# Two constants of an issue order: gate rows made, stored and broadcast from a later point, and turned rows of the second batch counted as ready later

## The chip, the cores and the metric

The kernel runs on one core of a Trainium2 chip. A core has a matrix engine (PE, with its weight loads shown as PEld), a vector engine (DVE), a scalar engine (ACT), a GpSimd engine (POOL) and a sync engine (SP). Each engine works through its own instruction queue in order and waits on semaphores that others raise. Transfers are issued from the queues of POOL, SP and ACT and are carried by 16 DMA engines that all of them share. The metric is the device time of one execution, in microseconds (us).

## The reference

Attention with 4 sink keys and a window of 128 keys, over 4 batches, 8 heads, 768 positions and 64 channels; its output, as 3072 rows of 512 channels, goes through a mixture of 4 experts that are all computed for every row and added with weights (gates) that each row brings.

```python
scores = scale * np.matmul(q, k.transpose(0, 1, 3, 2))
keep = (pos[None, :] < n_sink) | ((rel >= 0) & (rel < window))
a = softmax(np.where(keep, scores, -1e9)); x = np.matmul(a, v)
p = domain_probs / (domain_probs.sum(-1, keepdims=True) + 1e-09)
for e in range(E):
    out += p[:, e:e + 1] * (np.maximum(x @ w1[e], 0.0) @ w2[e])
```

## The kernel before

**Tiling.** A batch is cut into 6 blocks of 128 rows, and two blocks make a group g of 256 rows, so there are 12 pairs (b, g). Attention of a pair takes, for each of 4 pairs of heads: scores (L684), exponentials on ACT (L709), masks on DVE (L703 or L718), the product with the values (L743 and L750), a division by the row sum (L777, then L780 on DVE in batch 0 or L789 on ACT), and a turn to channel-major (L808 with a copy at L270 in batch 0, a transposing DMA from SP later). The four sink keys have products of their own (`sinks`, L645), which need a group's q and k rows already turned. In batch 0, PE turns q and k; from batch 1 on a transposing DMA from SP does (`turn_nat`, L246).

**Experts.** A first product (weights w1) makes the hidden rows H, a second one (w2) the output. The first two pairs, (0,0) and (0,1), are "early": their first products are plain (L1058) or of the seven-product form (L1145), without gates, and their second products (L1397) multiply by the gate while they leave PSUM (L1407, L1409 on DVE). All other pairs multiply by the gate while H leaves PSUM (L1082 after plain products, L1178 after seven-product ones); their gates lie along the free axis and are the same on all partitions. Their second products are L1319. The seven-product forms need sums of weights, formed on DVE (L377 to L383 for w1, L341 to L347 for w2). A part of those for expert 2 lies in the same buffer as `scratch`, in which the gates are normalized.

**The gate rows.** `gates_by_row` does four DVE instructions on 24 partitions (a sum, an addition, a reciprocal, a product, L434 to L437) and two stores from SP into a buffer in DRAM (L441). `load_gates` then broadcasts one row of 256 gates to 128 partitions from there, for each pair and expert, with one DMA from SP (L457, 128 KB). It has 5 buffers: the first five broadcasts are issued at once, each later one when a pair and expert is finished. So the five rows of the first call are those of pair (0,2) with experts 0 to 3 and of pair (1,0) with expert 0.

**What sets the order.** The program writes out every engine's instructions once, in an order that a planner in the kernel chooses. It keeps a clock for each engine and queue in `t`, in ns by costs of its own, and in each turn of the main loop it emits for PE the piece of work that is ready first or has the best priority. Work of DVE and ACT is put into `pend` with a ready time and a deadline, and `flush` emits it up to PE's clock. Times of DMAs are estimated too: `lands` for loads from POOL, `sp` for DMAs from SP. The planner's clock decides the order alone; on the chip the waits are on semaphores.

Three places matter here. The main loop calls the gate rows once PE's clock has passed a constant:

```python
        if not rowed and now > ROWED:
            rowed = 1
            gates_by_row()
            load_gates()
```

`gates_by_row` books 2989 ns of DVE on the planner's clock by `dve(2800, 0.0)`, and `load_gate` books the SP queue, but the time at which a gate row lands is kept nowhere: the work at L1082 and L1178 counts as ready when its product is. The third place is the time at which a turned block of q and k rows counts as ready:

```python
        turned_at[b, tb] = sp(landed["qk", b, tb], scored_at.get(b - 1, 0.0),
                              issue=1330, takes=1400, turning=True) + LATE + ROWS1 * (b == 1)
```

`scores_ready`, `sinks_ready` and the step `keys` read it, so for batch 1 alone `ROWS1` says how much later these steps may be emitted. It also sets when the buffers of q and k rows count as free (`qkn_free`), and with that when loads of batch 2 are emitted and when three of the buffers are taken for expert 3's sums of w2 (`spare_rows`).

**Loads.** POOL issues all loads of q, k, v and weights in one order. Around the change they are: w1 of expert 1, w2 of expert 1, w1 of 2, w2 of 2, w1 of 3, then rows of batch 1, with w2 of 3 between them. Each weight load puts 1 MB into SBUF.

Of the kernel before, what the change touches and what calls it, by code (L numbers as in the profile page):

```python
# [16 lines left out]
def kernel(  # L17
# [63 lines left out]
    OPEN = 2.2  # L81
    SOON = 21000
    NEARLY = 2
    ROWED = 24000
    W2AT = 2
    ROWS1 = 1500
    ONACT = 1
    ONE = 2
    PAIR = 1
# [107 lines left out]
    def sp(*deps, issue=530, takes=600, turning=False):  # L197
        t["sp"] = max([t["sp"], *deps]) + issue
        at = max(t["hw"], t["sp"] + 800)
        row = next((x[3] for x in moved if x[1] <= at < x[2]), 0.0)  # L200
        if turning and row:
            t["hw"] = at + TURNED * (row + SHARE)
            t["sw"] += TURNED * SHARE
            for x in moved:
                if x[2] > at:
                    x[1] += TURNED * SHARE * (x[1] > at)
                    x[2] += TURNED * SHARE
                    landed[x[0]] = x[2] + 900
                    if x[0][0] == "w1" and ("w1", x[0][1]) in landed:
                        landed["w1", x[0][1]] = max(landed["w1", x[0][1]], x[2] + 900)  # L210
        else:
            t["hw"] = at + takes + max(0.0, min(takes, t["sw"] - at)) * (not turning)
        return t["hw"] + 900
# [28 lines left out]
    def turn_nat(b, tb):  # L242
# [6 lines left out]
        )  # L249
        turned_at[b, tb] = sp(landed["qk", b, tb], scored_at.get(b - 1, 0.0), issue=1330, takes=1400, turning=True) + LATE + ROWS1 * (b == 1)  # L250
        qkn_free.remove(1e12)
# [1203 lines left out]
    while mix.more() or att.more():  # L1455
        now = t["pe"]

        if not att.more() and ahead == B - 1 and not wide:
            wide = 1
            mix.widened()  # L1460
        if not rowed and now > ROWED:
            rowed = 1
# [107 lines left out]
```

## Time and profile before

| | |
|---|---|
| median of 3 runs | 361.21 us (360.98 to 362.25) |
| profiled execution, first to last instruction | 361.5 us |
| busy: PE, DVE, ACT, POOL | 351.5, 303.8, 162.4, 71.7 us |
| granted PE clock, mean | 0.999 |
| moved by DMA | 37.79 MB, mean 105 GB/s |
| the chain that ended last | PE 86%, DMA 11%, DVE 1% |

The profile is of one execution. "x8" counts instructions; a bracket behind an instruction says how long its engine stood idle before it and what released it. In the lists of waits, the numbers are the total in us, the times, and the longest. A DMA in the chain is counted from its issue to its landing. PE is busy nearly all the time, so a gap on PE, or work on PE that could be left out, is what the time can be read from.

### The profile page before, as it was taken

How to read it: one execution, taken by the hardware profiler on the slowest of the kernel's cores; microseconds unless marked ns; L12 is line 12 of the kernel's file. 1: busy time of each engine (PE TensorE's matmuls, PEld its weight loads, DVE VectorE, ACT ScalarE, POOL GpSimd, SP SyncE). 2: the span in 40 equal slices, each digit the busy share in tenths (PEclk: the TensorE clock that was granted, in tenths of full speed). 3: DMA queues.
4: the chain of work that ended last, by engine and by line, in shares of the span. 5: the costliest groups of instructions: out<-in, count | busy, mean ns of one | idle time of the engine just before them, and what ended most of it. 6: DMA issues, size and time to landing. Idle time of an engine off the chain costs nothing.

```text
span 361.5 us, 10704 instructions
## 1 busy us (share of the span) xinstructions
PE 351.5 (97%) x4476; PEld 302.4 (84%) x4484; DVE 303.8 (84%) x691; ACT 162.4 (45%) x414; POOL 71.7 (20%) x92
## 2 busy tenths in 40 slices
PE   8999989998999999999999999999999999999995
PEld 3575758766789898898899898899899999999984
DVE  6787969868799899699579999989879799899840
ACT  5854722447694373554544435345344432313110
POOL 8936012540356224001071000000000000000000
PEclk9999999999999999999999999999999999999999
DMA  9999999999999999217099712121310131110011
GB/s 165 171 180 194 232 210 180 156 146 169 176 133 173 162 157 135 61 47 86 19 158 173 126 65 55 31 75 16 60 62 28 31 76 60 31 58 4 3 60 59
DMA packets 117869, 37.79 MB, mean 105 GB/s; under 512 B 100676, under 2 KB 113316, under 8 KB 117820
## 3 DMA queue, kind: packets, MB, share of 16 engines
q0 software_dynamic: 77520, 17.31, 54.0%
q1 hardware_dynamic: 39244, 19.28, 27.8%
q8 instruction: 35, 0.57, 0.6%
q10 hardware_dynamic: 1056, 0.52, 0.5%
q14 instruction: 14, 0.11, 0.1%
HBM read 40.98 MB, written 6.34 MB: 131 GB/s over the span
## 4 chain that ended last, share of the span: by engine, by line
PE 86%; DMA 11%; DVE 1%; issue 1%; ACT 1%; POOL 0%; ACTq 0%; POOLq 0%; DVEq 0%
PE acc L1319 34%; PE cps L1145 32%; DMA w<-in_moe_w_dram 9%; PE hps L1058 7%; PE acc L1397 6%; PE sps L684 3%; PE od L750 2%; DMA kraw<-in_k_dram 2%; PE od L743 1%; PE sinks L645 0%; ACT aT L709 0%; POOL w L312 0%; DVE qkn L345 0%; DVE qkn L343 0%; ACT qkn L270 0%
## 5 line engine op out<-in xcount | busy, mean ns | idle before, releaser
L1145 PEld LDWEIGHTS <-w 128*128 128x128 bf16 x1184 | 72.5, 98 | 2.3 <-issue 0.9
L1319 PEld LDWEIGHTS <-H 128*128 128x128 bf16 x700 | 65.0, 98 | 8.0 <-issue 1.5
L1178 DVE SCALAR_TENSOR_TENSOR H<-cps,gates 128x512 bf16<-128x512 f32 x90 | 60.3, 679 | 0.1
L709 ACT ACTIVATE aT<-sps 128x512 bf16<-128x512 f32 (+1 forms) x96 | 46.9, 573 | 24.7 <-PE sps L684 24.6
L1319 PE MATMUL acc<-w,H 128*128 128x256 bf16 x420 | 55.4, 273 | 0.0
L1145 PEld LDWEIGHTS <-vf 128*128 128x128 bf16 x744 | 45.6, 98 | 1.2 <-issue 0.5
L1145 PE MATMUL cps<-T,w 128*128 128x128 bf16 x592 | 45.0, 219 | 0.0
L1058 PE MATMUL hps<-xT,w 128*128 128x256 bf16 x352 | 43.3, 273 | 0.9 <-DMA w<-in_moe_w_dram 0.9
L1145 PE MATMUL cps<-xT,w 128*128 128x128 bf16 x592 | 43.7, 219 | 0.0
L789 ACT ACTIVATE onat<-od,R 128x64 bf16<-128x64 f32 x144 | 33.2, 323 | 22.7 <-DVE R L777 22.6
L1191 ACT COPY cps<-cps 128x512 f32<-128x512 f32 x37 | 21.4, 578 | 42.1 <-PE cps L1145 27.5
L1058 PEld LDWEIGHTS <-w 128*128 128x128 bf16 x352 | 33.3, 98 | 6.6 <-DMA w<-in_moe_w_dram 1.2
L1369 ACT COPY osb<-acc 128x256 f32<-128x256 f32 x36 | 13.6, 377 | 50.7 <-PE acc L1319 50.7
L1145 PE MATMUL cps<-T,vf 128*128 128x128 bf16 x496 | 36.4, 219 | 0.0
L299 POOL DMA_DIRECT2D vx<-in_v_dram x24 | 21.6, 905 | 62.2 <-PE od L750 48.5
L1319 PEld LDWEIGHTS <-S 128*128 128x128 bf16 x320 | 30.4, 98 | 3.3 <-issue 0.2
L1397 PE MATMUL acc<-w,H 128*128 128x512 bf16 x120 | 29.3, 379 | 2.0 <-DMA w<-in_moe_w_dram 1.3
L1198 DVE TENSOR_TENSOR cps<-H,cps 128x512 f32<-128x512 f32 x32 | 22.1, 691 | 9.8 <-PE cps L1145 8.4
L1319 PE MATMUL acc<-wf,H 128*128 128x256 bf16 x208 | 29.3, 273 | 0.0
L703 DVE TENSOR_TENSOR aT<-aT,mask 128x1024 bf16<-128x1024 bf16 (+1 forms) x36 | 22.7, 640 | 4.3 <-ACT aT L709 4.0
L1213 DVE TENSOR_TENSOR H<-H,cps 128x512 f32<-128x512 f32 x32 | 21.8, 680 | 2.7 <-PE cps L1145 2.6
L1397 PEld LDWEIGHTS <-H 128*128 128x128 bf16 x128 | 12.1, 98 | 13.5 <-issue 1.7
(128 smaller groups left out, 546.2 us busy)
## 6 DMA issues: line engine op xcount, KB each, us to landing
w<-in_moe_w_dram POOLq DMA_DIRECT2D x7, 1024.0 KB, 18.3
out_dram<-osb SPq DMA_DIRECT2D x21, 256.0 KB
gates<-gate_rows SPq DMA_DIRECT2D x40, 128.0 KB
vx<-in_v_dram POOLq DMA_DIRECT2D x24, 128.0 KB, 7.0
qkn<-in_q_dram POOLq DMA_DIRECT2D x22, 128.0 KB, 8.8
qkn<-in_k_dram POOLq DMA_DIRECT2D x22, 128.0 KB, 9.8
w<-in_moe_w_dram POOLq DMA_DIRECT2D x2, 512.0 KB, 9.4
kraw<-in_k_dram ACTq DMA_DIRECT2D x2, 256.0 KB
```

The lines of the kernel that those rows point to most:

```text
L299: nc.gpsimd.dma_start(out=vx[tb][:, :, 0:D], in_=v[b, :, tb * P:(tb + 1) * P, :].rearrange("h p d -> p h d"),)
L703: nc.vector.tensor_mul(a, a, m[:, None, :].to_broadcast([P, 2, w]))
L709: nc.scalar.activation(out=a[:, ph], in_=sps[ph][:, 0:w], func=AF.Exp, scale=scale)
L789: nc.scalar.mul(o[:, qi, hp, ph * D:(ph + 1) * D], od[:, qi, ph, 0:D], R[:, qi, ph])
L1058: nc.tensor.matmul(h[:, i].rearrange("p (q n) -> p q n", q=2), lhsT=w1_sb[e][:, db, fb * P:(fb + 1) * P], rhs=xT[b, g][:, :, db], start=(i ...
L1145: nc.tensor.matmul(y[:, f], lhsT=A[:, d, f * P:(f + 1) * P], rhs=T[:, d], start=(m in ("P1", "P5") and f == 0 and d == 0), stop=(d == 1), ...
L1178: nc.vector.scalar_tensor_tensor(out=dst, in0=src, scalar=0.0, in1=gate, op0=ALU.max, op1=ALU.mult)
L1191: nc.scalar.copy(out=tiles["Y"], in_=y)
L1198: nc.vector.tensor_add(tiles["V"], c5, tiles["X"])
L1213: nc.vector.tensor_add(c5, c5, y)
L1319: nc.tensor.matmul(x, lhsT=self.operand(b, g, e, m)[:, f], rhs=forms[e][m][:, f], start=(k == 0 and f == 0 and m in (("P1", "P5", "P2") if ...
L1397: nc.tensor.matmul(op, lhsT=H[:, fb // QF, fb % QF, s], rhs=w2_sb[e][:, fb, :], start=(fb == 0), stop=(fb == NFB - 1),)
```

## The change

Two constants differ.

```diff
-    ROWED = 24000
+    ROWED = 38000
     W2AT = 2
-    ROWS1 = 1500
+    ROWS1 = 3500
```

With the first, the four DVE instructions, the two stores and the first five broadcasts of the gate rows are emitted when PE's planning clock has passed 38 us, not 24 us. With the second, the planner counts each of the six turned blocks of q and k of batch 1 as ready 2 us later than it did. No instruction is added or taken away by either; what else moves is what the planner orders differently because of them.

## The prediction

> **What bounds the kernel now.** I read the page first: PE is busy 351.5 of 361.5 us, so the time is PE's work plus PE's gaps. The list of PE's waits for named work has four gaps from 0.8 us up; one is at 1.4 us, before any of this, and the others are
>
> ```profile
> PE acc L1397 <- DMA w<-in_moe_w_dram: 1.3, 1, 1.3
> PE hps L1058 <- DMA w<-in_moe_w_dram: 0.9, 1, 0.9
> PE sinks L645 <- DVE qkn L345: 0.8, 1, 0.8
> ```
>
> The second is at 19.7 us, before either constant acts. Where the other two lie is seen in PE's timeline (start, duration, and in brackets the idle time):
>
> ```profile
> 43.86 1.04 PE L1058 MATMUL hps<-xT,w 128*128 128x256 bf16 x8
> 46.21 1.89 PE L1397 MATMUL acc<-w,H 128*128 128x512 bf16 x7 [1.32 <-DMA w<-in_moe_w_dram]
> ...
> 87.99 0.61 PE L1145 MATMUL cps<-xT,w 128*128 128x128 bf16 x8
> 89.45 0.29 PE L645 MATMUL sinks<-qkT,ksd 128*32 128x256 bf16 x4 [0.85 <-DVE qkn L345]
> ```
>
> Ends of matmuls are modelled, so I count by starts. Eight of 256 columns start 0.109 us apart, so the products at 43.86 free PE at 44.73: that gap is 1.48 us. The eight at 87.99 are through at about 88.4: 1.05 us. After 90 us I find no start on PE more than 0.25 us late against its columns. These two gaps, 2.5 us in all, are about what any reordering can win.
>
> The first gap's cause is in the chain, in order of time; expert 1's w2 lands at 46.17:
>
> ```profile
> 27.91 18.26 DMA w<-in_moe_w_dram
> 46.17 0.04 issue
> 46.21 0.38 PE acc L1397
> ```
>
> The weight landings of this queue are at 37.67, 46.17, 51.07, 56.15 and 61.16 us, so this 1 MB took 8.50 us and the next three 4.90 to 5.08. In between lie the gate rows (SP's timeline) and a DMA rate over its surroundings (windows: length, PE, PEld, DVE, ACT, POOL busy, clock, DMA share, GB/s):
>
> ```profile
> 27.96 1.72 SPq L441 DMA_DIRECT2D gate_rows<-scratch  x2
> 34.66 2.28 SPq L457 DMA_DIRECT2D gates<-gate_rows  x5
> ```
> ```profile
> 30.00:38.00 8.00, 7.84 (x70) 4.11 (x70) 6.39 (x13) 4.05 (x9) 3.98 (x6) 1.00 1.20 208
> 38.00:46.00 8.00, 6.82 (x93) 5.83 (x90) 7.72 (x24) 5.39 (x10) 0.83 (x1) 1.00 1.16 236
> 46.00:56.00 10.00, 9.68 (x64) 6.39 (x66) 6.25 (x11) 1.79 (x3) 1.75 (x2) 1.00 1.19 211
> 55.95:69.35 13.40, 13.35 (x181) 11.66 (x181) 13.26 (x22) 6.14 (x11) 7.22 (x8) 1.00 1.71 177
> ```
>
> The packets of the five broadcasts run from 38.0 to 46.1 us and put down 0.65 MB; meanwhile POOL's queue falls from 206 GB/s to between 135 and 177. The last window matters below: DVE is busy 13.26 of 13.40 us there.
>
> For the second gap the named releaser is chance: the weight load of L645 waits for the semaphores of two transposing DMAs, and the one issued at 79.51 (block 3 of batch 1) lands at 89.31.
>
> **The change, part 1: ROWED.** I take from the planner's clock only the order. It passes 38 us at 38.1, just ahead of the reciprocal that the trace has at 39.24. DVE's lines:
>
> ```profile
> 24.94 0.67 DVE L434 TENSOR_REDUCE scratch<-scratch 24x128 f32<-24x512 f32 x1
> ...
> 26.87 1.07 DVE L437 TENSOR_TENSOR scratch<-scratch 24x512 f32<-24x512 f32 x1
> ...
> 39.24 0.17 DVE L777 RECIPROCAL R<-od 128x4 f32<-128x4 f32 x1
> ...
> 53.36 0.69 DVE L1082 SCALAR_TENSOR_TENSOR H<-hps,gates 128x512 bf16<-128x512 f32 x1 [0.40 <-PE hps L1058]
> 53.97 0.68 DVE L377 TENSOR_TENSOR vf<-w 128x1024 bf16<-128x1024 bf16 x1
> 55.09 0.75 DVE L1409 SCALAR_TENSOR_TENSOR osb<-acc,scale_t,osb 128x512 f32<-128x512 f32 x1 [0.44 <-PE acc L1397]
> ```
>
> Removed at 24.94: 3.0 us of DVE (24.94 to 27.94). DVE idles 0.82 us right after, waiting for PE, so nothing is won. Two stores and five broadcasts leave the weight queue's way: w2 of expert 1 should take 5.0 us as its neighbours do and land at 37.67 + 5.0 = 42.7, before PE's 44.73. Gain 1.48 us.
>
> Added at 39.24: the same 3.0 us of DVE, to 42.2. Behind it queue masks, divisions and turns of batch 0. PE need not stand: the planner books the work, and has first products of (0,0) and (0,1) of expert 1 to put forward (w1 landed at 37.67). DVE's idle times up to 55.1 (1.32, 0.65, 0.78, 0.40, 0.44) are 3.59 us, 2.1 of them left if PE is 1.48 earlier; alone the block would leave DVE 0.9 us behind. If that cover were gone PE would lose the whole 3.0.
>
> SP's queue is empty from 8.4 to 60.5 us but for these transfers, and POOL's loads wait for none of them; both cost nothing.
>
> What the planner doesn't know is the landing of the rows. Before, DVE ended at 27.94 and row 0 landed at 40.07: 12.1 us, of which 6.7 for the stores (4.0 from issue to first packet) and 5.4 for the broadcast (3.3 to first packet). From 42.2 that gives 54.3; if the stores start as quickly as the broadcasts did, which met the same large weight packets, 53.6, which I take as the nearest row. Its first reader is the L1082 at 53.36, due 1.48 earlier, at 51.9. So DVE stands for 1.7 us, with evictions L1409 and weight sums queued behind. At 53.6 it is 0.24 behind its old times, regains the 0.44 of idle at 55.09, and from 55.96 to 69.35 has no idle to give: 0.20 ahead. PE leans on it there: the sum L1198 ends at 62.26 and the product that reads it starts near 62.6, a tolerance of 0.3. So PE keeps 0.5 of its 1.48: part 1 is **-0.5 us**. Ends: -1.48 if the rows are in time; +3.1 if row 0 takes the longest broadcast of the trace (issued 70.35, landed 78.61: 8.3 us), so 42.2 + 6.7 + 8.3 = 57.2 and 57.2 - 53.36 - 0.44 - 0.3.
>
> [...]
>
> **Part 2: ROWS1.** No instruction is added. Keys, scores and sinks of batch 1 come up to 2 us later in the order. `sinks` of group 1 is emitted as soon as block 3 counts as ready, so up to 2 us of other PE work (early products, second products) moves ahead of it. PE then reaches it at 88.4 - 0.5 + 2.0 = 89.9, after 89.31: **-1.05 us**. Ends: +0.0 if the piece put ahead must wait itself, -1.4 with the 0.32 us late start behind the scores at 89.85. The masks (L703) and expert 3's weight sums shift too; cover is DVE's idle time between 88.60 and 97.20, 8.60 less 5.63 busy, 3.0 us. If they land beyond it, where DVE is busy 10.00 of 10 us (100 to 110), up to 3.0 us can come back. I take 0 for this, since with the same booking rules no other order-made gap is in the trace after 90 us.
>
> **Sum.** -0.5 - 1.05 = -1.55 us. The profiled span, 361.5, is 0.3 over the median; I see nothing around it to count. 361.21 - 1.55 = 359.7 us. Faster or slower by 0.5% means under 359.4 or over 363.0.
>
> **The rivals.** *In time* (0.24): row 0 lands before about 52.5, DVE stays with PE and both gaps close: 361.21 - 1.48 - 1.05 = 358.7. For it: the broadcast issued at 143.32 landed at 146.41, 3.1 us; with that for both steps and 1.7 us to issue the stores row 0 lands at 42.2 + 1.7 + 3.1 + 3.1 = 50.1. Against: weight loads keep the DMA engines at 211 GB/s from 46 to 56, against 92 from 140 to 150.
>
> *Given back* (0.26): DVE work moved by the new order meets the full stretches 55.95 to 69.35 or 100 to 120, and PE waits there what it won: between 360.5 and, with the 3.0 us, 362.7; I put it at 361.3. It includes that ROWS1 only swaps one late transfer for another. For it: DVE at 84% of the span; against: PE has products to do whenever DVE is behind.
>
> *Rows late* (0.14), the slower side: PE's change from row 0's landing L is L - 54.1, with part 2 L - 55.15; over 1.8 us from L = 57.0 on. At 57.2 it is 361.21 + 2.05 = 363.3. For it: the 8.3 us row, and 5.6 for the row issued at 60.48; against: the 8.3 stood behind two transposes on SP's queue, and there are none before 60 us.
>
> **Numbers.** The forecast itself gets 0.36, with 359.0 to 360.5 as its own range, some 0.10 of it under 359.4. Faster 0.24 + 0.10 = 0.34. Slower: rows late and 0.06 of given back, 0.20. Same 0.46. Range 358.4 (in time, with the 0.32) to 363.1.
>
> **What would show it.** Landing of expert 1's w2 near 42.7 and no PE gap before L1397 there: else the broadcasts weren't what slowed it. First L1082 waiting for a gates DMA until 53 to 54.5: if it doesn't wait, "in time" holds; past 57, "rows late". PE less than 0.8 us ahead at 70 us. No gap before `sinks` near 90 us. PE without gaps over 0.5 us after 97. I'm wrong if the planner puts waits of other kinds into the first 100 us, above all for turned rows or weight sums.

## The result and the profile after

| | median, us | range | ratio to before, 95% interval |
|---|---|---|---|
| before, beside it | 361.63 | 360.93 to 362.69 | |
| changed | 364.01 | 363.83 to 364.73 | 1.0072 (1.0055 to 1.0090) |

The changed kernel is 0.7%, some 2.4 to 2.6 us, slower: outside the range, and on the other side. The profiled execution took 364.6 us, with a span of 362.9 us.

PE's waits for named work are the first view (total in us, times, longest). The waits for `w` before L1397 and before `sinks` that before had are gone, and a new one stands at the top:

```profile
PE cps L1145 <- DVE H L1082: 2.1, 1, 2.1
PE acc L557 <- DVE lent L468: 1.4, 1, 1.4
```

The chain shows where it comes from, in order of time (start, duration): DVE's gate instructions, the store, the broadcast of row 0, the first L1082, three more of them among other DVE work, and PE's product.

```profile
40.59 1.07 DVE scratch L437
...
42.65 5.18 DMA gate_rows<-scratch
47.82 0.02 SPq L457
...
47.87 7.02 DMA gates<-gate_rows
...
54.99 0.13 DVE H L1082
...
61.33 0.61 DVE H L1082
61.94 0.04 issue
61.98 0.27 PE cps L1145
```

From DVE's end at 41.66 to row 0's landing at 54.89 it is 13.2 us. DVE's timeline (start, duration; in brackets the idle time before, and its releaser) shows what that does:

```profile
50.58 0.69 DVE L383 TENSOR_TENSOR w<-w 128x1024 bf16<-128x1024 bf16 x1
54.99 0.69 DVE L1082 SCALAR_TENSOR_TENSOR H<-hps,gates 128x512 bf16<-128x512 f32 x1 [3.72 <-DMA gates<-gate_rows]
55.60 0.68 DVE L343 TENSOR_TENSOR wf<-wf,w 128x1024 bf16<-128x1024 bf16 x1
...
57.46 0.68 DVE L1082 SCALAR_TENSOR_TENSOR H<-hps,gates 128x512 bf16<-128x512 f32 x1
...
60.05 0.68 DVE L1082 SCALAR_TENSOR_TENSOR H<-hps,gates 128x512 bf16<-128x512 f32 x1
...
61.24 0.69 DVE L1082 SCALAR_TENSOR_TENSOR H<-hps,gates 128x512 bf16<-128x512 f32 x1
```

DVE has nothing it may do for 3.72 us, because the wait stands at the head of its queue; then it works without a gap until 65 us. Each of the four L1082 reads a PSUM tile that PE's next products need: six PSUM banks go round in this part of the kernel. PE's timeline shows the stop, until the last of the four has read its bank:

```profile
59.32 0.61 PE L1145 MATMUL cps<-xT,w 128*128 128x128 bf16 x8
61.98 1.86 PE L1145 MATMUL cps<-T,vf 128*128 128x128 bf16 x16 [2.05 <-DVE H L1082]
```

By starts PE is 2.22 us late there, and it was 0.50 us late before, at 58.87, where the profile names ACT's copy L1191, itself released by the second L1082. Two landmarks on PE give the balance, first in before, then in the changed kernel:

```profile
55.76 1.89 PE L1397 MATMUL acc<-w,H 128*128 128x512 bf16 x8
68.36 1.89 PE L1397 MATMUL acc<-w,H 128*128 128x512 bf16 x7
```
```profile
53.56 1.89 PE L1397 MATMUL acc<-w,H 128*128 128x512 bf16 x8
70.06 1.89 PE L1397 MATMUL acc<-w,H 128*128 128x512 bf16 x7
```

PE came 2.2 us ahead and left 1.7 us behind, so 3.9 us were lost in between. The two late starts are 2.7 us of it. Another 1.4 us are slower products: from 61.98 to 70.06 the changed kernel takes 8.08 us for what took before 6.68 us (61.68 to 68.36). A product of 0.2 us (L1153) that before has in this stretch is not in the changed profile. `sinks` is reached at 93.42 without a wait, and after 97 us no start of PE is more than 0.25 us late.

The slower products have their reason in the clock. In a table of windows (length; busy PE, PEld, DVE, ACT, POOL; granted clock, DMA share, GB/s) PE's clock falls to half during the stop, at 61.53, and stays there for 3.41 us:

```profile
60.00:61.00 1.00, 0.00 (x0) 0.00 (x0) 1.00 (x3) 0.16 (x1) 0.91 (x2) 1.00 2.43 155
61.00:62.00 1.00, 0.02 (x1) 0.02 (x1) 1.00 (x3) 0.41 (x1) 0.90 (x2) 0.77 2.39 158
62.00:63.00 1.00, 1.00 (x11) 1.00 (x10) 1.00 (x2) 0.00 (x0) 0.73 (x2) 0.50 1.82 184
63.00:64.00 1.00, 1.00 (x12) 1.00 (x11) 1.00 (x3) 0.58 (x1) 1.00 (x2) 0.50 1.29 210
```

By its mean clock the profiled execution is one of two among six that had this. The four others are slower than before as well, 363.83 to 364.07 us.

### The profile page after: what moved, and what is told of

It reads as the page before. It is cut to its first block, busy times and chain, and to the rows that moved or that the text cites. A ratio compares the mean times of both kernels' runs of the same rounds, so it can differ in the third digit from the quotient of the medians.

```text
span 362.9 us, 10709 instructions
## 1 busy us (share of the span) xinstructions
PE 353.8 (98%) x4475; PEld 304.3 (84%) x4483; DVE 302.2 (83%) x687; ACT 163.8 (45%) x418; POOL 71.9 (20%) x92
## 4 chain that ended last, share of the span: by engine, by line
PE 88%; DVE 4%; DMA 3%; ACT 2%; issue 1%; SPq 0%; DVEq 0%; ACTq 0%
PE acc L1319 34%; PE cps L1145 32%; PE hps L1058 8%; PE acc L1397 5%; PE sps L684 3%; PE od L750 3%; DMA gates<-gate_rows 2%; PE acc L557 2%; DMA gate_rows<-scratch 1%; ACT aT L709 1%; PE od L743 1%; DVE onat L780 1%; PE tr L578 1%; DVE H L1082 1%; DVE aT L718 1%
## 5 line engine op out<-in xcount | busy, mean ns | idle before, releaser
L1191 ACT COPY cps<-cps 128x512 f32<-128x512 f32 x37 | 21.6, 585 | 44.1 <-PE cps L1145 27.7
L1198 DVE TENSOR_TENSOR cps<-H,cps 128x512 f32<-128x512 f32 x32 | 22.2, 693 | 10.5 <-PE cps L1145 8.8
L1397 PE MATMUL acc<-w,H 128*128 128x512 bf16 x120 | 29.2, 379 | 0.5 <-issue 0.2
L1397 PEld LDWEIGHTS <-H 128*128 128x128 bf16 x128 | 12.2, 98 | 12.1 <-issue 0.2
```

Source lines behind the costliest of these rows:

```text
L1191: nc.scalar.copy(out=tiles["Y"], in_=y)
L1198: nc.vector.tensor_add(tiles["V"], c5, tiles["X"])
L1397: nc.tensor.matmul(op, lhsT=H[:, fb // QF, fb % QF, s], rhs=w2_sb[e][:, fb, :], start=(fb == 0), stop=(fb == NFB - 1),)
```

## The experiments

The theory was: DVE's wait for a late gate row costs the time, and nothing else in the change does. The rivals were the DVE block in its new place, the half clock, and ROWS1.

**The kernel before once more, and each constant alone.** The first has no edit; the others change one constant each:

```diff
-    ROWED = 24000
+    ROWED = 38000
```
```diff
-    ROWS1 = 1500
+    ROWS1 = 3500
```

> Nothing is changed. Theory: in the profiled execution of before, the loads of the first 25 us came late (expert 0's w2 landed at 27.63, and at 25.95 in the changed kernel's profile, where nothing before 24 us differs), so the 1.48 us gap before L1397 at 46.21 belongs to that execution. Then this profile shows expert 0's w2 landing near 26, a gap under 0.6 us there, a span near 360, and the gap before the sinks of batch 1 (1.05 us) still there. Rival: the gap is the kernel's own, from the broadcasts alone: expert 1's w2 8.5 us after w1, a gap of 1.3 to 1.5 us, whatever the start.

> The gate rows from 38 us, ROWS1 as before. Theory (row 0 lands near 55, DVE waits for it 3 to 4 us in order and PE loses it between 58 and 65): all of the loss is here, and ROWS1's gain of 1.0 is missing: 2.4 + 1.0 = 3.4 us over before. Rival (the loss comes from batch 1's later order): within 0.7 us of before.

> ROWS1 alone, the gate rows from 24 us. Theory: the gap before the sinks closes and nothing else opens: 1.0 us under before (0.7 to 1.3). Rival (the later order of batch 1 fills stretches in which DVE is full, and costs): 1 to 2.5 us over before.

| | median, us | ratio, 95% interval |
|---|---|---|
| before | 362.08 | |
| before again | 361.84 | 1.0003 (0.9988 to 1.0019) |
| ROWED alone | 364.51 | 1.0067 (1.0045 to 1.0088) |
| ROWS1 alone | 361.01 | 0.9978 (0.9962 to 0.9994) |

ROWED alone brings the loss, 0.67% (2.4 us), and its DVE timeline has the same wait:

```profile
51.08 0.69 DVE L383 TENSOR_TENSOR w<-w 128x1024 bf16<-128x1024 bf16 x1
55.62 0.69 DVE L1082 SCALAR_TENSOR_TENSOR H<-hps,gates 128x512 bf16<-128x512 f32 x1 [3.85 <-DMA gates<-gate_rows]
```

ROWS1 alone is 0.22% faster, 0.8 us by the ratio, and its profile has no gap before `sinks`. But the 3.4 us expected of ROWED alone did not come: the two constants together (1.0072) lose as much as ROWED alone (1.0067), so the gain of ROWS1 does not show beside a late row. In the profile of ROWED alone PE reaches `sinks` at 91.11 without a wait; it comes there so late that ROWS1 has no gap to close. The half clock is in this number too: five of the six executions of ROWED alone have it by their mean clock, with spans of 362.6 to 363.5 us, and the one without has 361.6 us. How much of the 2.4 us it is can't be told from one execution.

The new profile of before is the other finding. Its span is 359.5 us in an execution of 361.23 us, and PE's waits in it are:

```profile
PE acc L557 <- DVE lent L468: 1.4, 1, 1.4
PE sinks L645 <- DMA qkT<-qkn: 0.6, 1, 0.6
```

The second line names the transposing DMA as what `sinks` waits for, as the prediction had argued. The wait for w2 of expert 1, which the prediction meant to win back, is not there: w2 landed at 44.02, just ahead of PE. An execution takes its span and about 1.7 us (1.65 to 1.77 in 75 executions of before). The profiled execution of before, with 361.5 us of span, had therefore, worked out so, taken about 363.2 us, 1.6 to 2 us over the median. The gap comes and goes: four profiles have the gate rows from 24 us, and three of them have it (before, ROWS1 alone with 1.0 us in its list of waits, and the kernel below that does the DVE block twice, with 1.4 us). What repeats is the slow load behind it: in these four, w2 landed 7.2 to 8.5 us after w1. In the seven profiles with the rows from 31 us or later it landed 5.1 to 5.9 us after w1, and none has the gap.

**The rows in time.** The same edit, but at an earlier point, with ROWS1 at 3500:

```diff
-    ROWED = 38000
+    ROWED = 31000    # and 34500, and 36000
```

> The gate rows from 31 us, ROWS1 3500. Theory: DVE ends them near 35, row 0 lands 12 to 13 us later, near 48, before its first reader at 51 to 52: no wait of DVE for a gate row, the broadcasts mostly behind expert 1's w2. Time as ROWS1 alone or a little better, 1.0 to 1.7 us under before. Rival (it is the 3 us block on DVE amid batch 0's last masks, not the landing, that costs): 1 us or more over before.

> The gate rows from 34.5 us, ROWS1 3500. DVE ends them near 38, so row 0 lands near 51, about when its first reader comes (51.3). Theory (the cost begins where the landing passes the reader, and PE has some slack behind that): 0.5 to 1.2 us under before. Rival (the cost grows with every us of delay from 31 to 38): halfway, 0.7 us over before or more.

> ROWS1 at 3500, ROWED at 36000. On the queues this is the changed kernel with the DVE block about 1.7 us (one eviction, one reciprocal, one division, one mask) further ahead; the order behind it is nearly the same. The theory (PE pays for the time that DVE waits for row 0, and the row lands about 13.2 us after the block's end) expects the block's end near 40.0 us, row 0 near 53.2, DVE waiting for about 2.0 us instead of 3.7 before the first L1082, and the time 1.7 us under the changed kernel's: 0.3 to 1.0 us over the kernel before. The rival (the block's place behind 37 us, not the row's landing, is what costs) expects the changed kernel's time: 2.0 us or more over the kernel before.

The start of the two stores on SP, the landing of row 0 where a wait shows it, DVE's idle time that a gate row ends, and the time (each ratio is to executions of before beside that run):

| ROWED | stores from | row 0 lands | DVE waits | median, us | ratio, 95% interval |
|---|---|---|---|---|---|
| 31000 | 35.53 | in time | 0 | 361.00 | 0.9972 (0.9959 to 0.9984) |
| 34500 | 38.07 | in time | 0 | 360.73 | 0.9970 (0.9960 to 0.9980) |
| 36000 | 39.97 | 52.54 | 1.36 | 361.45 | 0.9990 (0.9978 to 1.0003) |
| 38000 | 41.68 | 54.89 | 3.72 | 364.01 | 1.0072 (1.0055 to 1.0090) |

At 34500 the first L1082 starts without a wait; at 36000, where DVE's order is nearly that of the changed kernel, it has a short one. DVE's timelines, of 34500 and then of 36000:

```profile
51.47 0.68 DVE L1082 SCALAR_TENSOR_TENSOR H<-hps,gates 128x512 bf16<-128x512 f32 x1
```
```profile
50.59 0.68 DVE L383 TENSOR_TENSOR w<-w 128x1024 bf16<-128x1024 bf16 x1
52.64 0.69 DVE L1082 SCALAR_TENSOR_TENSOR H<-hps,gates 128x512 bf16<-128x512 f32 x1 [1.36 <-DMA gates<-gate_rows]
```

So the loss follows the row, not the move. Against 34500 the later points cost 0.20% (0.7 us) for 1.36 us of DVE's wait and 1.02% (3.7 us; 3.3 us by the medians) for 3.72 us. The forecast for 36000 was 0.3 to 1.0 us over before, and it came out 0.1% under: the row came 0.7 us earlier than I had worked out, and by the ratios, whose intervals just touch, PE forgives about half of a wait of this length. The rival's 2.0 us or more is excluded, and so are the rivals' 0.7 and 1 us over before for 34500 and 31000, which came out 1.0 to 1.1 us under, as the theory had it. 34500 beats both kernels, and it scatters less than before: 360.43 to 361.34 us in 12 executions, against 361.08 to 363.12 in the 29 of before beside it.

**The DVE block without the late rows.** The rows are made and stored at 24000 as before, and the four DVE instructions are done a second time at 38000, on the same data and without stores; ROWS1 is 3500:

```diff
-    def gates_by_row():
+    def gates_by_row(stored=True):
...
-        for i in range(2):
+        for i in range(2 * stored):
...
+        if rowed == 1 and now > 38000:
+            rowed = 2
+            gates_by_row(False)
```

> ROWS1 3500; the gate rows made, stored and broadcast from 24 us, and the same four DVE instructions (3.0 us) done a second time from 38 us, where the changed kernel has them, with nothing stored. Theory (the landing of row 0 costs, not the DVE block): as ROWS1 alone, 0.5 to 1.2 us under before, no idle of DVE before its first L1082. Rival (3 us of DVE amid batch 0's last masks cost by themselves): 1 us or more over before.

Measured: 361.87 us, 1.0003 (0.9990 to 1.0016). That lies between the two expectations. Beside ROWS1 alone (0.9978) the 3 us of DVE cost about 0.25%, 0.9 us, with intervals that overlap. Its profile has no wait for gate rows, and between 36 and 120 us the only start of PE that is over 0.25 us late is the one that waits for w2 before L1397 (1.6 us). So the profile shows no wait of PE that the block made; whether the block costs anything is not resolved. Either way a block of 3 us of DVE costs PE far less than a DVE that must not move.

**A planner that knows when the rows land.** The changed kernel, but the clock of the planner holds back work on the first five rows until they are due:

```diff
+        gate_at[pair, e] = t["pe"] + 15400 + 1000 * len(gate_sb) if len(gate_sb) < NGATE else 0.0
...
-            later("dve", end, GATE0, run)
+            later("dve", max(end, gate_at[b * NG + g, e]), GATE0, run)
...
-                later("dve", ready, slack, run)
+                later("dve", max(ready, gate_at[b * NG + g, e]), slack, run)
```

> The changed kernel, but the planner books the landing of the first five gate rows (15.4 us after their issue, 1 us more for each next one) and counts the gated evictions as ready no earlier. The rows land as late as before. Theory (what costs is that DVE stands in order before the first L1082, with evictions and weight sums behind it): DVE does other work first, its idle before L1082 falls from 3.7 to under 1 us, and the time lies between 1.0 us under and 0.8 us over the kernel before. Rival (the late rows cost by the PSUM banks that wait for them, whatever the order): 2 us or more over before.

Measured: 362.91 us, 1.0023 (1.0011 to 1.0035). Weight sums and L1409 now go ahead of the gated work, and DVE waits 0.68 us in place of 3.72:

```profile
54.78 1.29 DVE L1083 SCALAR_TENSOR_TENSOR H<-hps,gates 128x512 bf16<-128x512 f32 x2 [0.68 <-DMA gates<-gate_rows]
```

(One line was added ahead of it, hence L1083.) By the ratio that is 0.8 us over before (0.4 to 1.3), the upper end of what the theory allowed; the rival's 2 us or more is excluded. The ratio falls from 1.0072 to 1.0023, half of the way to the 0.9970 of rows in time. PE's starts are still late by 0.42, 0.69 and 0.63 us between 58 and 64 us, and by 0.54, 0.45 and 0.31 us between 96 and 102 us. The profile names ACT's copy of a product and twice DVE's sum of two as what the first three waited for, and two gated evictions (L1179) and a mask for the last three. Whether it is the banks, held by tiles that wait for their gates, wasn't tested.

**The half clock.** The changed kernel with ten products of zeros, 512 columns each, into an accumulator that is free then, just before the product that stood waiting:

```diff
             elif m == "P5":
+                for _ in range(10 if (b, g, e) == (0, 0, 2) else 0):
+                    nc.tensor.matmul(acc[0], lhsT=zeros[:, 0:P], rhs=zeros, start=True, stop=True)
```

> The changed kernel with ten products of zeros (2.1 us) on PE into an output bank that is free there, just ahead of the product at which PE stands still for 2.2 us; they are not on the planner's clock, so the order is the same. Theory (the standstill makes the granted clock fall to half for 3.4 us in a part of the executions, 363.0 us of span with it and 362.1 without): no execution has the half clock at 61 to 65 us, and the time is 0.3 to 0.9 us under the changed kernel's, 1.5 to 2.1 over before. Rival (the clock falls for another reason or costs nothing, since DVE sets the pace there): the half clock stays, 2.4 us over before.

Measured: 364.14 us, 1.0071 (1.0051 to 1.0092). In the profile PE is busy and the clock full where the changed kernel had it empty and halved:

```profile
60.00:61.00 1.00, 1.00 (x6) 0.49 (x5) 1.00 (x2) 0.33 (x1) 0.89 (x2) 1.00 2.43 155
61.00:62.00 1.00, 1.00 (x9) 0.48 (x7) 1.00 (x3) 0.24 (x1) 0.92 (x2) 1.00 2.41 156
62.00:63.00 1.00, 1.00 (x22) 1.00 (x20) 1.00 (x3) 0.54 (x1) 0.92 (x2) 1.00 1.90 181
```

Yet the median is that of the changed kernel, and the 0.3 to 0.9 us that the theory expected did not come. Four of the six executions of the changed kernel have a full clock anyway (mean 0.998 to 1.0) and spans of 362.1 to 362.4 us; the two with a mean of 0.994 have 362.9 and 363.0 us. So the loss is there without the half clock, and the half clock adds 0.5 to 0.9 us where it comes. With the zeros, five executions have spans of 362.1 to 362.7 us. The sixth has a mean clock of 0.995 and 364.4 us (366.09 us of time, the longest of all): the theory's "no execution has the half clock" failed too, or the clock fell somewhere else in it, for which there is no trace.

DVE is busy 1.00 of 1.00 us in all of these windows, with zeros as without. In the profile with zeros PE spends 2.2 us on them and starts late by 0.33, 0.47 and 0.31 us around it: 3.3 us lost at full clock, for a wait of DVE of 3.55 us.

## Why the prediction was wrong

**The step that failed** is part 1. It had -0.5 us for ROWED; ROWED alone measured +0.67%, 2.4 us. The sum let row 0 land at 53.6, DVE stand for 1.7 us, and PE keep 0.5 us of a gain of 1.48. In the runs row 0 landed at 54.89, DVE stood for 3.72 us, and PE lost nearly all of that, while the gain of 1.48 comes to some 0.3 us, not resolved, where the rows are in time. That a late row would stop DVE in order was foreseen; its size was not.

**The base.** "These two gaps, 2.5 us in all" were read from one execution, and "I see nothing around it to count" was wrong: 1.7 us lie around the span. The profiled execution was about 2 us over the median, and most of that was the 1.48 us gap, which another profile of the same kernel doesn't have. So the -1.48 of part 1 could not be taken from the median in full. With the rows in time, part 1 wins 0.06 to 0.08% over ROWS1 alone (0.9972 and 0.9970 against 0.9978), some 0.3 us and not resolved by the intervals. The mechanism of the slow load held: w2 of expert 1 landed 5.12 us after w1 in the changed kernel (35.93, 41.05), where 5.0 was predicted and before's profile had 8.50.

**Row 0.** The step "53.6, which I take as the nearest row", with DVE standing for 1.7 us, failed by 2.0 us. The row came at 54.89: DVE's end was 0.5 us earlier than worked out, but the two transfers took 13.2 us, where I had chosen 11.4 over the 12.1 that the profile of before showed for the same two steps. DVE was free for the reader, due at 51.9, at 51.27. In the second profile of before the reader starts at 51.34, 2.0 us earlier than in the first, and 1.48 us of that was all I had taken off. The broadcast alone took 7.0 us from issue to landing (47.87 to 54.89), where the profile of before has 5.4.

**PE's tolerance.** "PE leans on it there: the sum L1198" named a dependency that was not the one that cost. What PE ran into were banks read by L1082: 0.50 us by way of ACT's copy, then 2.22 us for the last of the four. (At 36000, where the wait is short, two of PE's three late starts, 0.47 and 0.31 us, do stand behind L1198.) The four L1082 all queue behind the same wait, among 0.7 us pieces of other DVE work that had also been held up. The 2.1 us of idle time that DVE had before 55 us were counted as reserve for the block, and they could be none for a wait behind which everything queues.

**The rival.** "Rows late" had the right mechanism and the right side, with 0.14. Its price, L - 54.1, gives +0.8 us at L = 54.89, where the trace has +1.7 at 70 us, and that against an execution of before that was itself about 2 us over the median. Its turning point, L = 57.0, was therefore too late by more than 2 us: 54.9 was enough for +2.4, and at 52.5 the change came out even.

**Part 2**, taken alone, was right in kind and near in size: -1.05 predicted, -0.8 us measured, and no gap before `sinks`. No 3.0 us came back later on. But it was not a term that could be added to part 1: with PE late behind row 0 the gap closes by itself, and ROWS1 won nothing there. (A slip without consequence: after 90 us one start, at 90.23, is 0.32 us late; part 2 uses it, while the text on the gaps says none over 0.25.)

## What to carry to other kernels

- A gap in one profile is worth its length only if the profiled execution is a typical one: set span and surroundings against the median first, and where a landing decides the gap by a microsecond, expect it to come and go.
- Moving the start of a chain of transfers later is paid for at the first in-order reader, since that engine can do nothing behind the wait. Here a wait of 1.36 us cost about 0.7 us, and one of 3.72 us nearly all of it (3.3 us by the medians). Take the longest measured time of the chain, not the kindest row, and put the step as late as the reader's due time less that (here 34.5 us instead of 38 us).
- Where an issue order is planned on a clock that doesn't know a landing, an idle engine's reserve is no cover for that landing.

## What the runs showed of the hardware

PE's granted clock fell to 0.50 for 3.41 us, from 61.53 in the changed kernel's profile and from 63.53 in that of ROWED alone. Each has one stop of PE of 2.2 us there. In the first the clock fell 1.8 us into the stop, in the second 0.9 us behind its end; in the 3.41 us before the fall PE had products for 1.1 and 1.2 us. It did so only in some of the executions: two of six of the changed kernel and five of six with ROWED alone have a mean clock of 0.994 or 0.995. What makes the clock fall, and how long a stop it takes, these runs don't show: with zeros in place of the stop the granted clock is 1.00 from 60 to 66 us in the profile, but one of six executions has a mean of 0.995.
